# Moving 272 TensorE transposes of an attention + MLP kernel to the DMA crossbar on SyncE's queue

## The chip, the cores and the metric

The kernel runs on one core of one Trainium2 chip. The metric is device time in microseconds (us) of one execution; lower is better. Where a number below comes from several executions it is a median with its range. Each run was profiled too, and the profile gives the "span", from the first to the last counted instruction; it is 1 to 3 us shorter than the time.

The engines are TensorE (PE; its weight loads are PEld), VectorE (DVE), ScalarE (ACT), GpSimd (POOL) and SyncE (SP), which in this kernel only issues DMAs. Lines such as L216 are lines of the kernel's source. The changed kernel has other line numbers than the kernel before, since lines were added.

## The reference

Sliding-window causal attention, then a residual MLP with a layer norm in front:

```python
# q, k, v: (8, 8, 576, 64) = batch, head, position, head dim, float32; window = 64
scores = q @ k.T / sqrt(64);  keep 0 <= i - j < 64
attn = softmax(scores) @ v                       # (8, 8, 576, 64)
x = attn.transpose(0, 2, 1, 3).reshape(8, 576, 512)
xn = (x - mean) / sqrt(var + 1e-6) * g_ln
out = x + relu(xn @ w_ch1) @ w_ch2               # 512 -> 2048 -> 512
```

## The kernel before

The work is cut into nine groups. Group g runs the MLP of batch g's first 512 positions (group 8: the 64 last positions, the "tail", of all eight batches). While PE does the MLP of batch g, the kernel also does the attention of batch g+1 and prepares q, k and v of batch g+2. The MLP of a group is a list of 30 units (16 pieces of layer 1, called `l1` or `hps`, then 14 stages of layer 2), and the other work is placed behind units by slot numbers. The program gives each engine its instructions in the order of these slots, and the timelines below show them run in that order.

Three things are transposed. In the kernel before, PE does it against an identity matrix, and ACT or DVE copies the result out of PSUM: q and k of each batch (`t_main`), q and k of the tails (`t_tail`), and the normalised rows z that feed layer 1 (`zt_step`).

```python
def load_qk(b, half):
    for x, src in enumerate((q, k)):
        t = p_in.tile([128, 1024], FP32, tag=f"qk32_{x}", ...)          # 2 buffers
        ...
        nc.sync.dma_start(                                              # 512 KB, runs of 1 KB
            out=t[:, :].rearrange("p (h m) -> p h m", h=4),
            in_=src[b, 4*half:4*half+4, 0:SM, :].rearrange("h (p j) d -> p h (j d)", j=4))

def t_main(b, x, half, eng=None):
    src = qk16.pop((b, x, half))
    tp = t_tile([128, 8, 128], ...)                                     # PSUM
    for i in range(8):
        nc.tensor.transpose(out=tp[:, i, :], in_=src[:, i], identity=ident16)
    ...
    evac(x if eng is None else eng, dst..., tp...)                      # ACT or DVE copy

def zt_step(g, kb, eng="act"):
    z = zsd.pop((g, kb))
    ...                                                                 # zT[g]: [128, 4, 512] fp16
    ztp = t_tile([128, NKC, 128], ...)
    for kc in range(NKC):
        nc.tensor.transpose(out=ztp[:, kc, :], in_=z[:, 128*kc:128*(kc+1)], identity=ident16)
    dst = zT[g][:, :, 128*kb:128*kb+128]
    nc.scalar.copy(out=dst, in_=ztp)

def l1(hc):                                       # needs ALL of zT[g]
    for kc in range(NKC):
        nc.tensor.matmul(out=hps, lhsT=w1g[:, kc, 128*hc:128*(hc+1)], rhs=zT[g][:, kc, :], ...)

def b_step(g, kb):                                # attention output -> x_norm, pool pxn: 4 buffers
    if kb % 2 == 0:
        x_norm[(g, kb // 2)] = p_xn.tile([128, 2, DM], FP32, tag="xn", ...)
    ...

def store(kb):                                    # the same buffer, after the MLP was added to it
    nc.sync.dma_start(out=out[g, 128*kb:128*kb+128, :], in_=x_norm[(g, kb // 2)][:, kb % 2, :])

# schedule of group g (b = g + 1, n = g + 2); TAILS = {3: [0], 5: [1], 7: [2, 3]}; cut
at((2, 7, 12, 17)[j], z_step, b, j)               # z on POOL, four blocks
at((8, 13, 18, 23)[j], zt_step, b, j)
for i, (x, half) in zip((17, 19, 21, 25), ...): at(i, t_main, n, x, half, 0)
at(17, load_qk, n + 1, 0);  at(18, load_qk, n + 1, 1);  at(23, load_v, n + 1, 0, 4)
# tail i of the next group: load_tail at 5, cast_tail at 24, t_tail at 27 and 29
# its first use: s_mm of the tail at slot 1 of groups 3, 5 and 7
# stores: two in stage "4", two in stage "3" (the last four units)
```

All loads and stores of this schedule and (after the change) all crossbar transposes are issued by SyncE; of the large transfers only the copies that make vB (GpSimd's queue) and one 128 KB store (ScalarE's) are not. The timelines show SyncE issuing in order: an issue that has to wait for its input holds up everything that SyncE would issue after it (experiment 9 shows one such wait, 3.4 us).

The softmax here doesn't subtract the row's maximum and nothing guards it: scores larger than these inputs give would overflow.

Of the kernel before, what the change touches and what calls it, by code (L numbers as in the profile page):

```python
# [11 lines left out]
FP16 = mybir.dt.float16  # L12
# [8 lines left out]
def kernel(  # L21
# [10 lines left out]
    nc = tc.nc  # L32
    B, H, S, D = q.shape
    DM = H * D
    HID = 4 * DM
    SM = 512
# [2 lines left out]
    NHC = HID // 128  # L39
    NHP = H // 2  # L40
    EPS = 1e-6
    scale = 1.0 / (D ** 0.5)

    p_const = ctx.enter_context(tc.tile_pool(name="pconst", bufs=1))
    p_wst = ctx.enter_context(tc.tile_pool(name="pwst", bufs=4))
    p_in = ctx.enter_context(tc.tile_pool(name="pin", bufs=2))
# [25 lines left out]
    def t_tile(shape, name):  # L72
        i = 0 if tbank["shared"] else tbank["n"] % 2
        tbank["n"] = i + 1
        return ps_t.tile(shape, FP16, tag=f"t{i}", name=name)

    qk32, qk16, v32 = {}, {}, {}
    tail32, tail16, tailT, vT = {}, {}, {}, {}
    qkT, vA, vB, pts = {}, {}, {}, {}
    x_norm, zT, mvg, zsd, rstd = {}, {}, {}, {}, {}  # L80

    def load_qk(b, half):
        for x, src in enumerate((q, k)):
            t = p_in.tile([128, 1024], FP32, tag=f"qk32_{x}", name=f"qk32_{x}_{b}_{half}")
            qk32[(b, x, half)] = t
            if b < 2:
                nc.sync.dma_start(  # L87
                    out=t[:, :].rearrange("p (h m) -> p h m", h=H),
                    in_=src[b, :, 256 * half:256 * half + 256, :].rearrange("h (p j) d -> p h (j d)", j=2),
                )  # L90
            else:
                nc.sync.dma_start(
                    out=t[:, :].rearrange("p (h m) -> p h m", h=4),
                    in_=src[b, 4 * half:4 * half + 4, 0:SM, :].rearrange("h (p j) d -> p h (j d)", j=4),
                )
# [12 lines left out]
    def cast_tail(i):  # L108
        tq, tk, tv = tail32.pop(i)
        q16 = p_in.tile([128, H, D], FP16, tag="tq16", name=f"tq16_{i}", bufs=1)  # L110
        k16 = p_in.tile([128, 2, H, D], FP16, tag="qk16_1", name=f"tk16_{i}")
        vt = p_va.tile([128, 2, H, D + 1], FP16, tag="vt", name=f"vt_{i}", bufs=1)
        tail16[i] = (q16, k16)
        vT[i] = vt
        nc.gpsimd.memset(vt[:, :, :, D:D + 1], 1.0)
        nc.gpsimd.tensor_copy(out=q16, in_=tq)
        nc.gpsimd.tensor_copy(out=k16, in_=tk)
        nc.gpsimd.tensor_copy(out=vt[:, :, :, 0:D], in_=tv)

    def cast_qk(b, half):  # L120
        for x in range(2):
            t = qk32.pop((b, x, half))
            dst = p_in.tile([128, 8, 2, D], FP16, tag=f"qk16_{x}", name=f"qk16_{x}_{b}_{half}")
            qk16[(b, x, half)] = dst
            j = 2 if b < 2 else 4
            nc.gpsimd.tensor_copy(  # L126
                out=dst[:, :].rearrange("p (a j) e d -> p a e j d", j=j),
                in_=t[:, :].rearrange("p (a e j d) -> p a e j d", e=2, j=j, d=D),
            )
# [70 lines left out]

    def alloc_qkT(b):
        qkT[b] = [p_qkt.tile([128, NHP, SM + 64 * x], FP16, tag=f"qkT{x}", name=f"qkT{x}_{b}") for x in range(2)]
        nc.gpsimd.memset(qkT[b][1][:, :, 0:64], 0.0)

    def evac(x, out, in_):
        if x == 0:
# [2 lines left out]
            nc.vector.tensor_copy(out=out, in_=in_)  # L209

    def t_main(b, x, half, eng=None):
        src = qk16.pop((b, x, half))
        j = 2 if b < 2 else 4
        tp = t_tile([128, 8, 128], f"tp_{b}_{x}_{half}")
        for i in range(8):
            nc.tensor.transpose(out=tp[:, i, :], in_=src[:, i], identity=ident16)  # L216
        if b < 2:
            c0 = 64 * x + 256 * half
            dst = qkT[b][x][:, :, c0:c0 + 256]
        else:  # L220
            dst = qkT[b][x][:, 2 * half:2 * half + 2, 64 * x:64 * x + 512]
        evac(x if eng is None else eng, dst.rearrange("c h (p j) -> c h p j", j=j),
             tp[:, :].rearrange("c (h j) p -> c h p j", j=j))

    def t_tail(i, x):
        src = tail16[i][x]
        if x == 0:
            tailT[i] = (p_qkt.tile([128, NHP, 128], FP16, tag="tqT", name=f"tqT_{i}", bufs=1),
                        p_qkt.tile([128, 2, NHP, 128], FP16, tag="tkT", name=f"tkT_{i}", bufs=1))
            tp = t_tile([128, NHP, 128], f"tpq_{i}")  # L230
            for hp in range(NHP):
                nc.tensor.transpose(out=tp[:, hp, :], in_=src[:, 2 * hp:2 * hp + 2, :], identity=ident16)
        else:
            tp = t_tile([128, 2, NHP, 128], f"tpk_{i}")
            for r in range(2):
                for hp in range(NHP):
                    nc.tensor.transpose(out=tp[:, r, hp, :], in_=src[:, r, 2 * hp:2 * hp + 2, :], identity=ident16)
        evac(0, tailT[i][x], tp)

    def s_mm(g, j, pe_mask=False):  # L240
        sc = [ps_s.tile([128, NHP, 2, 64], FP32, tag="sc", name=f"sc_{g}_{j}_{par}") for par in range(2)]
        pt = p_pt.tile([128, 2, NHP, 2, 64], FP16, tag="pt", name=f"pt_{g}_{j}")
        pts[(g, j)] = pt
        if pe_mask:
            m = mbias[:, :]
            mb = bass.AP(tensor=m.tensor, offset=m.offset, ap=[m.ap[0], [0, NHP * 2], m.ap[1]])
            for par in range(2):
                nc.tensor.matmul(
                    out=sc[par][:, :].rearrange("p h w i -> p (h w) i"), lhsT=ident16, rhs=mb,
                    start=True, stop=False, skip_group_check=True,  # L250
                )
        for hp in range(NHP):
            for iw in range(2):
                for par in range(2):
                    rows = slice(64 * par, 64 * par + 64)
                    if g == NGRP - 1:
                        lhsT = tailT[j][1][rows, iw, hp, :]
                        rhs = tailT[j][0][rows, hp, 64 * iw:64 * iw + 64]
                    else:
                        w = 2 * j + iw  # L260
                        lhsT = qkT[g][1][rows, hp, 64 * w:64 * w + 128]
                        rhs = qkT[g][0][rows, hp, 64 * w:64 * w + 64]
                    nc.tensor.matmul(out=sc[par][:, hp, iw, :], lhsT=lhsT, rhs=rhs,  # L263
                                     start=not pe_mask, stop=True, skip_group_check=pe_mask)
        for par in range(2):
            nc.scalar.activation(out=pt[:, par], in_=sc[par], func=AF.Exp, bias=0.0, scale=scale)  # L266
# [54 lines left out]
    def zt_step(g, kb, eng="act"):  # L321
        z = zsd.pop((g, kb))
        if g not in zT:
            sfx = "r" if g == NGRP - 1 else ""
            zT[g] = p_grp.tile([128, NKC, 512], FP16, tag="zT" + sfx, name=f"zT_{g}", bufs=1 if sfx else 2)
        ztp = t_tile([128, NKC, 128], f"ztp_{g}_{kb}")
        for kc in range(NKC):
            nc.tensor.transpose(out=ztp[:, kc, :], in_=z[:, 128 * kc:128 * (kc + 1)], identity=ident16)  # L328
        dst = zT[g][:, :, 128 * kb:128 * kb + 128]
        if eng == "act":  # L330
            nc.scalar.copy(out=dst, in_=ztp)  # L331
        else:
            nc.vector.tensor_copy(out=dst, in_=ztp)
# [303 lines left out]
    for g in range(NGRP):  # L637
# [3 lines left out]
        def at(i, f, *a):  # L641
            slots[min(i, len(slots) - 1)].append((f, a))

        b = g + 1
# [78 lines left out]
        if g > 1 and b < B:  # L723
            for j in range(4):
                if j:
                    at((2, 7, 12)[j - 1], s_mm, b, j)
                    at((3, 8, 13)[j - 1], s_mask, b, j)
                at((2, 7, 12, 17)[j], b_step, b, j)
                at((2, 7, 12, 17)[j], z_step, b, j)
                at((8, 13, 18, 23)[j], zt_step, b, j)  # L730
        for n, i in enumerate(TAILS.get(g, ())):
            ts = (10, 11, 14, 20) if n else (1, 2, 5, 11)
            at(ts[0], s_mm, NGRP - 1, i)
# [5 lines left out]
        if g > 1 and n < B:  # L739
            at(16, cast_qk, n, 1)  # L740
            at(20, alloc_v, n)
            at(20, cast_v, n, 0, 2)
            at(21, cast_v, n, 2, 4)
            at(21, alloc_vB, n)
            at(21, make_vB, n)
            for i, (x, half) in zip((17, 19, 21, 25), ((0, 0), (1, 0), (0, 1), (1, 1))):
                at(i, t_main, n, x, half, 0)
            at(27, s_mm, n, 0)
            at(28, s_mask, n, 0)
            if n + 1 < B:  # L750
                at(17, load_qk, n + 1, 0)
                at(18, load_qk, n + 1, 1)
                at(23, load_v, n + 1, 0, 4)
# [53 lines left out]
```

## Time and profile before

| | before |
|---|---|
| time, median of 2 runs | 324.88 us (324.31 to 325.46) |
| span of the profiled run | 322.6 us |
| PE busy | 309.6 us (96%) |
| span less PE busy | 13.0 us |
| PE transposes | 448 |

The page of the kernel before opens with busy time and share of the span by engine, then shows busy tenths in 40 slices of the span. PEclk is the granted TensorE clock in tenths of full speed, DMA the mean busy share of the 16 DMA engines.

```profile
PE 309.6 (96%) x3229; PEld 204.6 (63%) x3229; DVE 204.3 (63%) x388; ACT 176.8 (55%) x292; POOL 164.6 (51%) x251
...
PE   7978999999989999999999999999999999999993
...
PEclk9999999999999999999999999999999999999998
DMA  8999999976089947904598459000570190003013
```

PE is busy in nearly every slice and its clock is full nearly throughout (mean 0.996); no other engine is near its limit. The chain of work that ended last says the same (shares of the span):

```profile
PE 85%; DVE 4%; SPq 3%; DMA 2%; POOL 2%; ACT 1%; issue 0%; ACTq 0%; POOLq 0%
```

So time taken off PE shortens this kernel, provided that PE does not wait for whatever takes the work over. What the transposes cost PE is read from the chain, in order of time (start, us, engine, output, line, count):

```profile
154.37 0.45 PE tp L216 x8
```

Eight transposes take 0.45 us of the chain, 0.056 us each. The groups of instructions (count, then busy us and mean ns of one, then idle before) show 225 ns each for the same instructions; that is how long one lasts, and they overlap, so the mean must not be multiplied by the count:

```profile
L216 PE MATMUL tp<-ident,qk 128*128 128x128 f16 x256 | 20.1, 225 | 0.0
```

The queue that the change uses is SyncE's. This is its timeline from 146 to 170 us (start, us, queue, line, operation, count); the duration is time that SyncE spent on the issue, waiting included:

```profile
147.81 0.39 SPq L92 DMA_DIRECT2D qk<-in_q_dram  x1
148.80 0.39 SPq L92 DMA_DIRECT2D qk<-in_k_dram  x1
...
158.82 4.68 SPq L139 DMA_DIRECT2D v<-in_v_dram  x4
163.68 4.14 SPq L401 DMA_DIRECT2D out_dram<-xn  x4
```

Per group it carries four loads of q and k, four of v and four stores; nothing stands on it that waits for the attention of this group. The list of waits holds one line that becomes important later (total us, times, longest):

```profile
DVE xn L297 <- DMA out_dram<-xn: 2.2, 3, 1.7
```

VectorE may write a new `x_norm` only once the store of the one that lay in that buffer has landed. In the kernel before that costs 2.2 us of DVE time and no visible PE time.

### The profile page before, as it was taken

The numbers are of one execution on the slowest core, as the hardware profiler recorded it, in microseconds if no ns is written. First come the engines' busy times: TensorE is split into PE (matmuls) and PEld (weight loads), VectorE is DVE, ScalarE is ACT, GpSimd is POOL, SyncE is SP. The second block draws the span as 40 slices with busy tenths as digits, with TensorE's granted clock in tenths as the row PEclk, the third lists the DMA queues.
The fourth block names the chain that finished last, engine by engine and source line by source line (L and its number), as shares of the span: only waits on it lengthen the run. The fifth ranks groups of instructions, "written<-read, shape, count | busy, mean of one in ns | idle before, by whom it ended". The sixth has DMA issues, their size and how long they took to land.

```text
span 322.6 us, 7813 instructions
## 1 busy us (share of the span) xinstructions
PE 309.6 (96%) x3229; PEld 204.6 (63%) x3229; DVE 204.3 (63%) x388; ACT 176.8 (55%) x292; POOL 164.6 (51%) x251
## 2 busy tenths in 40 slices
PE   7978999999989999999999999999999999999993
PEld 4556444687544578656964696459755865694582
DVE  0887764666885795489447954896559644751643
ACT  2576624487346754876457647775486157405600
POOL 7678765423991689079705982598036506200000
PEclk9999999999999999999999999999999999999998
DMA  8999999976089947904598459000570190003013
GB/s 194 282 385 259 363 306 295 264 267 133 35 276 227 207 139 204 241 2 133 173 259 183 132 168 259 26 2 2 171 182 2 24 241 33 0 2 131 0 36 98
DMA packets 85639, 51.08 MB, mean 158 GB/s; under 512 B 55682, under 2 KB 76674, under 8 KB 85603
## 3 DMA queue, kind: packets, MB, share of 16 engines
q1 hardware_dynamic: 84816, 48.11, 55.6%
q0 software_dynamic: 640, 2.33, 3.1%
q8 instruction: 25, 0.41, 0.5%
q10 hardware_dynamic: 146, 0.13, 0.1%
q14 instruction: 12, 0.09, 0.1%
HBM read 38.80 MB, written 9.44 MB: 150 GB/s over the span
## 4 chain that ended last, share of the span: by engine, by line
PE 85%; DVE 4%; SPq 3%; DMA 2%; POOL 2%; ACT 1%; issue 0%; ACTq 0%; POOLq 0%
PE hps L363 33%; PE pA L435 11%; PE pC L435 8%; PE pB L435 8%; PE hph L484 6%; PE ch L375 4%; PE xps L291 4%; PE tp L216 3%; PE sc L263 3%; DMA w1s<-in_moe_w_ch_dram 2%; PE ztp L328 2%; SPq L139 2%; POOL w1g L188 1%; PE ch L499 1%; DVE wT L532 1%; SPq L87 1%
## 5 line engine op out<-in xcount | busy, mean ns | idle before, releaser
L363 PE MATMUL hps<-zT,w1g 128*128 128x512 f16 x480 | 112.0, 379 | 0.0
L367 ACT ACTIVATE hrT<-hps 128x512 f16<-128x512 f32 x120 | 71.9, 599 | 35.1 <-PE hps L363 31.6
L363 PEld LDWEIGHTS <-w1g 128*128 128x128 f16 x480 | 44.1, 98 | 47.0 <-issue 1.0
L316 POOL TENSOR_SCALAR rsz<-mvg 128x1 f32<-128x1 f32 x28 | 12.2, 437 | 76.5 <-DVE mvg L302 75.5
L266 ACT ACTIVATE pt<-sc 128x512 f16<-128x512 f32 x72 | 39.0, 595 | 14.6 <-PE sc L263 13.1
L435 PEld LDWEIGHTS <-sS 128*128 128x128 f16 x448 | 43.0, 98 | 4.7
L207 ACT COPY qkT<-tp 128x1024 f16<-128x1024 f16 x26 | 26.2, 1012 | 33.6 <-PE tp L216 32.4
L126 POOL CAST qk<-qk 128x1024 f16<-128x1024 f32 x32 | 33.7, 1070 | 9.5 <-DMA qk<-in_q_dram 4.9
L442 DVE TENSOR_TENSOR xn<-pA,xn 128x512 f32<-128x512 f32 x28 | 19.2, 686 | 26.1 <-PE pA L435 17.4
L331 ACT COPY zT<-ztp 128x512 f16<-128x512 f16 x36 | 21.1, 586 | 26.5 <-PE ztp L328 26.1
L435 PEld LDWEIGHTS <-hrT 128*128 128x128 f16 x336 | 32.3, 98 | 5.0
L294 DVE RECIPROCAL rcp<-xps 128x8 f32<-128x8 f32 x36 | 7.4, 205 | 34.3 <-PE xps L291 34.1
L414 DVE TENSOR_TENSOR sS<-hrT 128x512 f16<-128x512 f16 (+1 forms) x42 | 21.4, 510 | 10.2 <-ACT hrT L367 10.2
L297 DVE TENSOR_TENSOR xn<-xps,rcp 128x512 f32<-128x512 f32 x36 | 24.9, 692 | 3.3 <-DMA out_dram<-xn 2.2
L435 PE MATMUL pA<-wT,sS 128*128 128x256 f16 x224 | 26.9, 273 | 0.0
L435 PE MATMUL pC<-w2s,sS 128*128 128x256 f16 x224 | 26.8, 273 | 0.0
L273 DVE TENSOR_TENSOR pt<-pt,mask 128x1024 f16<-128x1024 f16 x28 | 21.2, 762 | 8.6 <-ACT pt L266 8.5
L484 PE MATMUL hph<-zT,w1g 128*128 128x256 f16 x192 | 23.6, 273 | 2.5 <-ACT zT L331 1.1
L299 DVE BATCH_NORM_STATS2 stats<-xn 128x6 f32<-128x512 f32 x36 | 25.0, 695 | 1.2
L319 POOL TENSOR_SCALAR z<-xn,rsz 128x512 f16<-128x512 f32 x28 | 23.4, 836 | 2.9
L375 PE MATMUL ch<-w2s,hrT 128*128 128x512 f16 x96 | 23.7, 380 | 0.1
L484 PEld LDWEIGHTS <-w1g 128*128 128x128 f16 x192 | 18.0, 98 | 5.8 <-issue 2.2
(85 smaller groups left out, 437.2 us busy)
## 6 DMA issues: line engine op xcount, KB each, us to landing
out_dram<-xn SPq DMA_DIRECT2D x34, 256.0 KB, 3.6
qk<-in_q_dram SPq DMA_DIRECT2D x16, 512.0 KB, 4.8
qk<-in_k_dram SPq DMA_DIRECT2D x16, 512.0 KB, 5.9
v<-in_v_dram SPq DMA_DIRECT2D x32, 256.0 KB, 6.2
w2s<-in_moe_w_ch_dram SPq DMA_DIRECT2D x12, 512.0 KB, 5.6
w1s<-in_moe_w_ch_dram SPq DMA_DIRECT2D x4, 512.0 KB, 7.3
tk<-in_k_dram SPq DMA_DIRECT2D x8, 256.0 KB, 4.4
tv<-in_v_dram SPq DMA_DIRECT2D x8, 256.0 KB, 5.1
```

What stands on the lines that cost most here:

```text
L126: nc.gpsimd.tensor_copy(out=dst[:, :].rearrange("p (a j) e d -> p a e j d", j=j), in_=t[:, :].rearrange("p (a e j d) -> p a e j d", e=2, j ...
L207: nc.scalar.copy(out=out, in_=in_)
L266: nc.scalar.activation(out=pt[:, par], in_=sc[par], func=AF.Exp, bias=0.0, scale=scale)
L297: nc.vector.tensor_tensor(out=xn, in0=xps[:, :, 0:D], in1=rcp_b, op=ALU.mult)
L299: nc.vector.bn_stats(out=stats, in_=xv)
L319: nc.gpsimd.tensor_scalar(out=z, in0=xv, scalar1=rs, scalar2=nm, op0=ALU.mult, op1=ALU.add)
L363: nc.tensor.matmul(out=hps, lhsT=w1g[:, kc, 128 * hc:128 * (hc + 1)], rhs=zT[g][:, kc, :], start=(kc == 0), stop=(kc == NKC - 1),)
L367: nc.scalar.activation(out=hrT[:, hc, :], in_=hps, func=AF.Relu, bias=0.0, scale=1.0)
L375: nc.tensor.matmul(out=ch[kb], lhsT=hrT[:, hc, 128 * kb:128 * (kb + 1)], rhs=w2s[:, hc, :], start=(hc == 0), stop=(hc == NHC - 1),)
L414: nc.vector.tensor_tensor(out=o, in0=x, in1=y, op=op)
L435: nc.tensor.matmul(out=bank[which][:, p, :], lhsT=a[:, c, 128 * p:128 * p + 128], rhs=wv[:, c, :], start=(first and p == 0 and c == 0), st ...
L484: nc.tensor.matmul(out=hps[:, e], lhsT=w1g[:, kc, 128 * hc:128 * (hc + 1)], rhs=zT[g][:, kc, 256 * half:256 * half + 256], start=(kc == 0) ...
```

## The change

The intent: give PE less to do. From batch 4 on q and k are transposed by the DMA crossbar, one transpose of 512 KB for each of the two (`XQ = 4`); so are all tails, and the z of groups 3 to 8 (`XZ = 3`). That takes 272 of the 448 transposes from PE and 48 copies from ACT. For these transposes q and k lie in another layout, so their loads become eight of 256 KB in runs of 256 bytes in place of four of 512 KB in runs of 1 KB. The z transposes are placed one or two slots earlier, the q, k transposes all behind unit 17.

```diff
+    XQ = 4
+    XZ = 3
@@ load_qk
+            elif b >= XQ:
+                for c in range(2):
+                    s0 = 256 * half + 128 * c
+                    nc.sync.dma_start(
+                        out=t[:, 512 * c:512 * c + 512].rearrange("p (h d) -> p h d", h=H),
+                        in_=src[b, :, s0:s0 + 128, :].rearrange("h s d -> s h d"),
+                    )
@@ t_main
+        if b >= XQ:
+            if half == 0:
+                dst = flat(b, x)[:, 64 * x:64 * x + NHP * SM]
+                nc.sync.dma_start_transpose(out=dst.rearrange("p (a t) -> p a t", t=128),
+                                            in_=cast16[x][:, :, :, :].rearrange("p a c m -> p (a c m)"))
+            return
@@ t_tail, for q (x == 0); the same for k into tailT[i][1]
+            if XQ < B:
+                nc.sync.dma_start_transpose(out=tailT[i][0], in_=src[:, :, :].rearrange("p h d -> p (h d)"))
+                return
@@ zt_step
+        if g >= XZ:
+            nc.sync.dma_start_transpose(out=zT[g][:, :, 128 * kb:128 * kb + 128], in_=z)
+            return
@@ schedule
-                at((8, 13, 18, 23)[j], zt_step, b, j)
+                at((6, 11, 16, 22)[j], zt_step, b, j)
-            for i, (x, half) in zip((17, 19, 21, 25), ((0, 0), (1, 0), (0, 1), (1, 1))):
+            for i, (x, half) in zip((17, 17, 17, 17) if n >= XQ else (17, 19, 21, 25),
+                                    ((0, 0), (1, 0), (0, 1), (1, 1))):
```

Cut from the diff: static fp16 tiles `cast16` as the source of the transposes, the casts that write them in the new order, and the flat addressing of `qkT` in the score matmuls.

More of the change, by code (lines that the diff above doesn't have):

```diff
@@ L77 @@
     qk32, qk16, v32 = {}, {}, {}
+    cast16 = [p_const.tile([128, NHP, 4, 128], FP16, tag=f"cast16_{x}", name=f"cast16_{x}") for x in range(2)]
     tail32, tail16, tailT, vT = {}, {}, {}, {}
@@ L110, in cast_tail @@
         q16 = p_in.tile([128, H, D], FP16, tag="tq16", name=f"tq16_{i}", bufs=1)
-        k16 = p_in.tile([128, 2, H, D], FP16, tag="qk16_1", name=f"tk16_{i}")
+        k16 = cast16[1][:, 0:2].rearrange("p r c (e d) -> p r (c e) d", d=D)
         vt = p_va.tile([128, 2, H, D + 1], FP16, tag="vt", name=f"vt_{i}", bufs=1)
@@ L122, in cast_qk @@
             t = qk32.pop((b, x, half))
-            dst = p_in.tile([128, 8, 2, D], FP16, tag=f"qk16_{x}", name=f"qk16_{x}_{b}_{half}")
+            if b >= XQ:
+                nc.gpsimd.tensor_copy(
+                    out=cast16[x][:, :, 2 * half:2 * half + 2, :].rearrange("p a c m -> p c a m"),
+                    in_=t[:, :].rearrange("p (c a m) -> p c a m", c=2, a=NHP),
+                )
+                continue
+            dst = cast16[x][:, 2 * half:2 * half + 2, :, :].rearrange("p a c (e d) -> p (a c) e d", d=D)
             qk16[(b, x, half)] = dst
@@ L202, in alloc_qkT, with flat @@
         qkT[b] = [p_qkt.tile([128, NHP, SM + 64 * x], FP16, tag=f"qkT{x}", name=f"qkT{x}_{b}") for x in range(2)]
-        nc.gpsimd.memset(qkT[b][1][:, :, 0:64], 0.0)
+        if b < XQ:
+            nc.gpsimd.memset(qkT[b][1][:, :, 0:64], 0.0)
+        else:
+            nc.gpsimd.memset(qkT[b][1][:, 0, 0:64], 0.0)
+    def flat(b, x):
+        return qkT[b][x][:, :, :].rearrange("p h m -> p (h m)")
     def evac(x, out, in_):
@@ L211, in t_main @@
     def t_main(b, x, half, eng=None):
+        if b >= XQ:
+            if half == 0:
[3 more added lines that the diff above has]
+            return
         src = qk16.pop((b, x, half))
@@ L233, in t_tail @@
         else:
+            if XQ < B:
+                nc.sync.dma_start_transpose(out=tailT[i][1][:, :, :, :].rearrange("p r h t -> p (r h) t"),
+                                            in_=src[:, :, :, :].rearrange("p r h d -> p (r h d)"))
+                return
             tp = t_tile([128, 2, NHP, 128], f"tpk_{i}")
@@ L258, in s_mm @@
                         rhs = tailT[j][0][rows, hp, 64 * iw:64 * iw + 64]
+                    elif g >= XQ:
+                        c0 = SM * hp + 64 * (2 * j + iw)
+                        lhsT = flat(g, 1)[rows, c0:c0 + 128]
+                        rhs = flat(g, 0)[rows, c0:c0 + 64]
                     else:
@@ L325, in zt_step @@
             zT[g] = p_grp.tile([128, NKC, 512], FP16, tag="zT" + sfx, name=f"zT_{g}", bufs=1 if sfx else 2)
+        if g >= XZ:
+            nc.sync.dma_start_transpose(out=zT[g][:, :, 128 * kb:128 * kb + 128], in_=z)
+            return
         ztp = t_tile([128, NKC, 128], f"ztp_{g}_{kb}")
```

## The prediction

> **What bounds it now.** The page: PE is busy 309.6 of 322.6 us (96%) and holds 85% of the chain of waits; DVE has 63%, ACT 55%, POOL 51%. In the stretches from 131 to 305 us PE is 100% busy; groups 2 to 5 take about 33 us each. So a PE instruction removed there shortens the kernel, if its replacement arrives in time. The DMA share is about 0.76 between 148 and 198 us, lower later.
>
> **Removed.** 272 of 448 PE transposes (128 of q and k, 48 of tails, 96 of z) and 48 ACT copies. On the chain eight transposes cost 0.45 us, so PE loses 272 x 0.056 = 15.3 us, all on the critical path: about 3 us in each of groups 2 to 5, 1.6 and 1.1 in 6 and 7. ACT loses about 37 us, off the path.
>
> **Added.** On SyncE's queue: 8 transposes of 512 KB, 4 of 256 KB, 28 of 128 KB or so. The Trainium skill (DMA: Bandwidth & Descriptors, Latency and other measured facts) gives 261 GB/s for a DMA transpose; no run here shows it yet. Estimate: 2 us for 512 KB, 0.5 us for 128 KB, plus about 2 us latency (loads here start moving about 2 us after issue). The q, k loads of batches 4 to 7 break into 256-byte pieces: traced packets take 18 ns for 256 B, 46 ns for 1 KB, and v's 256-byte traffic moves about 800 packets/us, so one batch's q and k (8192 packets) take about 10 us, where the 2 MB took about 5.5 us.
>
> **Order on the queue decides.** SyncE issues in order, and each DMA engine takes a queue's descriptors in order (same page, Queues, rings and completion order). In groups 2 to 4 the order is: transposes of q, k; eight loads of the next batch; the transpose of z's last block; v loads; stores; tail transposes.
> - The casts that feed the q, k transposes end about 21 us into a group (POOL's timeline: 120.2, start 98.9). Add 4 to 5 us of transposes, 10 us of loads, 2 us of vB copies on POOL's queue, 1.5 us for z: the last zT block lands 37 to 39 us into the group. The next group's first matmul needs it; PE would arrive after 30.
> - tkT, needed two units (2 us) into groups 3, 5, 7, stands behind v (5 us), stores (2.8 us) and tqT: another 6 to 8 us of stall in groups 3 and 5, 3 to 4 in group 7.
>
> Sum: -15 saved, +24 (three z stalls of 8), +18 (tails): about +27.
>
> **Prediction:** 350 us, range 326 to 378. Faster 0.10, within 2% 0.08, slower 0.82.
>
> **What would show it.** PE busy falls by about 15 us yet the span grows; new PE waits at the first hps of groups 3, 4, 5 released by DMA zT<-z, and at the tail sc of groups 3, 5, 7 released by DMA tkT; eight load issues on SyncE between the q, k transposes and the fourth z transpose; groups without loads (5, 6) 2 to 3 us shorter; ACT busy 37 us less.
>
> **What would make it wrong.** Loads and transposes overlapping rather than draining in order, or 256-byte loads faster than v's: the z stall vanishes and 310 to 318 us follows. Transposes far slower than 261 GB/s (3x: 512 KB in 6 us), or long issue on SyncE: up to 390 us. A granted clock that falls in the new PE pauses adds more.

## The result

| | before | after |
|---|---|---|
| time, median (range, 2 runs each) | 324.88 us | 371.79 us (370.40 to 373.19) |
| span of the profiled run | 322.6 us | 371.4 us |
| PE busy | 309.6 us | 307.4 us |
| span less PE busy | 13.0 us | 64.0 us |
| PE transposes | 448 | 176 |
| ACT busy | 176.8 us | 143.4 us |
| packets of 256 bytes | 53,248 | 120,832 |
| mean granted TensorE clock | 0.996 | 0.919 |

The changed kernel is slower: ratio 1.144, 95% interval 1.124 to 1.165. Here and below, a ratio is the mean time of one kernel's fast runs over that of the other's fast runs of the same rounds, so it is not quite the ratio of the medians that are quoted. The single runs (experiments 1, 2, 4 and 7) have no known state, and a difference from them of a few us alone would show nothing; their traces carry the argument.

The sum closes exactly: PE busy changed by -2.2 us, PE's idle time by +51.0 us, together the +48.8 us of the span. The same lines of the page as before, now of the changed kernel:

```profile
PE 307.4 (83%) x2957; PEld 192.6 (52%) x2957; DVE 201.7 (54%) x388; ACT 143.4 (39%) x244; POOL 163.2 (44%) x251
...
PE   7989999999899804999349981389999975999994
...
PEclk9999999999999975699959996579999996999998
DMA  8999999654999999016999199911695194203013
...
PE 55%; SPq 16%; DVE 11%; DMA 6%; issue 6%; POOL 4%; ACT 1%; POOLq 0%; ACTq 0%
```

PE has holes, and in and after each hole the granted clock falls. The DMA share is 0.9 or more over most of the middle. In the chain PE fell from 85% to 55%, and SyncE's queue, 3% before, has 16%. PE's timeline shows the holes (in brackets: idle just before, and what ended it):

```profile
139.54 3.57 PE L405 MATMUL hps<-zT,w1g 128*128 128x512 f16 x8 [11.01 <-issue]
148.26 0.61 PE L302 MATMUL sc<-tqT,tkT 64*128 64x64 f16 x16 [5.15 <-DMA tkT<-cast]
...
190.72 4.80 PE L405 MATMUL hps<-zT,w1g 128*128 128x512 f16 x11 [10.99 <-issue]
...
233.96 3.57 PE L405 MATMUL hps<-zT,w1g 128*128 128x512 f16 x8 [10.04 <-DMA zT<-z]
242.95 0.61 PE L302 MATMUL sc<-tqT,tkT 64*128 64x64 f16 x16 [5.42 <-DMA tkT<-cast]
...
310.90 0.61 PE L302 MATMUL sc<-tqT,tkT 64*128 64x64 f16 x16 [6.98 <-DMA tkT<-cast]
```

Six pauses, 49.6 us in all: 32.0 us at the first layer-1 matmul of groups 3, 4 and 5, which needs the whole of zT, and 17.6 us at the tail scores of groups 3, 5 and 7. For two of the three zT pauses the profile names no releaser ("issue"). But the last zT transpose of group 4's rows landed at 190.63 us and PE went on at 190.72; for group 3's it was issued at 135.62, the last of the 16 increments of its semaphore is recorded at 139.45, and PE went on at 139.54.

Why zT comes so late is seen in SyncE's timeline of the changed kernel from 169 to 195 us, to be compared with that of the kernel before:

```profile
169.14 1.19 SPq L366 DMA_TRANSPOSE zT<-z  x1
170.42 4.47 SPq L237 DMA_TRANSPOSE qkT<-cast  x2
174.95 1.60 SPq L97 DMA_DIRECT2D qk<-in_q_dram  x2
176.59 2.11 SPq L97 DMA_DIRECT2D qk<-in_k_dram  x2
178.75 6.04 SPq L97 DMA_DIRECT2D qk<-in_q_dram  x2
184.83 1.96 SPq L97 DMA_DIRECT2D qk<-in_k_dram  x2
186.89 1.64 SPq L366 DMA_TRANSPOSE zT<-z  x1
188.63 2.98 SPq L155 DMA_DIRECT2D v<-in_v_dram  x4
191.70 2.73 SPq L443 DMA_DIRECT2D out_dram<-xn  x4
```

The transposes of z's third block and of its last block stand 17.8 us apart, with the q, k transposes and the next batch's eight loads between them. The last block of z was ready long before; POOL's timeline:

```profile
173.16 1.01 POOL L358 TENSOR_SCALAR z<-xn,rsz 128x512 f16<-128x512 f32 x1
```

It was made at 174.17 and its transpose issued at 186.89, 12.7 us later (in group 2: 122.98 and 135.62). The Trainium skill (DMA: Bandwidth & Descriptors, Queues, rings and completion order) says that on each DMA engine descriptors are consumed in ring order; this trace agrees: the transpose issued at 186.89 landed 3.7 us later, at 190.63, behind the last of those loads (190.08), where the median zT transpose needs 2.5. The eight loads keep SyncE itself for 11.7 us, up to 6 us for one pair of issues, where one of the four loads of the kernel before took it 0.4 us. In that stretch (174.95 to 186.80) the view of windows gives a DMA share of 1.13 (I read 1 or more as full engines). So order puts z behind the loads, and loads that fill the DMA engines make the place behind them expensive.

The view of DMA issues of the changed kernel gives the median time in us from issue to landing of the transposes of z and of q, k (the lines give no size; by the tiles they are 128 KB and 512 KB):

```profile
zT<-z SPq DMA_TRANSPOSE x24, 2.5
...
qkT<-cast SPq DMA_TRANSPOSE x8, 4.5
```

From 128 KB in 2.5 us to 512 KB in 4.5 us, 384 KB (393,216 bytes) more take 2.0 us longer, which is 197 GB/s. This slope includes SyncE's own time for the issue (median 1.2 us for zT, 2.1 for qkT), so it is not the rate of the transfer alone. From the list of waits of the changed kernel, for comparison with the experiments, the line of the `x_norm` buffers:

```profile
DVE xn L336 <- DMA out_dram<-xn: 0.6, 1, 0.6
```

Two things in the sum are less plain.

- PE busy fell by only 2.2 us although 15.3 us of transposes had gone. The granted clock was 0.5 in four stretches of the trace, in which PE was busy 25.4 us together. At full clock that would have been 12.7 us (this takes all PE work as going with the clock). So -15.3 and +12.7 leave 0.4 us of the measured -2.2 open.
- A group that loads nothing did get shorter. Group 6 runs 28.8 us from its first to its next group's first layer-1 matmul in the changed kernel (273.2 to 302.0), 30.5 us in the kernel before (231.3 to 261.8). So PE does profit where nothing stands in the queue.

### The profile page after: what moved, and what is told of

Its sections match the earlier page's. It is cut to its first block, busy times and chain, and to the rows that moved or that the text cites. A ratio compares the mean times of both kernels' runs of the same rounds, so it can differ in the third digit from the quotient of the medians.

```text
span 371.4 us, 7324 instructions
## 1 busy us (share of the span) xinstructions
PE 307.4 (83%) x2957; PEld 192.6 (52%) x2957; DVE 201.7 (54%) x388; ACT 143.4 (39%) x244; POOL 163.2 (44%) x251
## 4 chain that ended last, share of the span: by engine, by line
PE 55%; SPq 16%; DVE 11%; DMA 6%; issue 6%; POOL 4%; ACT 1%; POOLq 0%; ACTq 0%
PE hps L405 26%; SPq L97 6%; PE pA L477 6%; PE hph L526 5%; PE pC L477 4%; PE pB L477 4%; DMA tkT<-cast 4%; SPq L155 3%; PE ch L417 3%; PE xps L330 3%; PE sc L302 3%; SPq L443 2%; DMA w1s<-in_moe_w_ch_dram 2%; DVE stats L338 2%; DVE xn L336 2%
## 5 line engine op out<-in xcount | busy, mean ns | idle before, releaser
L405 PE MATMUL hps<-zT,w1g 128*128 128x512 f16 x480 | 119.6, 405 | 32.0 <-issue 22.0
L405 PEld LDWEIGHTS <-w1g 128*128 128x128 f16 x480 | 46.7, 102 | 89.7 <-issue 44.4
L477 PEld LDWEIGHTS <-hrT 128*128 128x128 f16 x336 | 32.5, 98 | 5.4
L312 DVE TENSOR_TENSOR pt<-pt,mask 128x1024 f16<-128x1024 f16 x28 | 23.4, 843 | 14.9 <-ACT pt L305 14.8
L358 POOL TENSOR_SCALAR z<-xn,rsz 128x512 f16<-128x512 f32 x28 | 24.4, 870 | 2.9
L142 POOL CAST cast<-qk 128x1024 f16<-128x1024 f32 x16 | 16.6, 1044 | 9.9 <-DMA qk<-in_q_dram 4.8
L526 PEld LDWEIGHTS <-w1g 128*128 128x128 f16 x192 | 18.1, 98 | 5.1 <-issue 2.2
L356 POOL TENSOR_TENSOR rsz<-rsz,mhalf 128x1 f32<-128x1 f32 x28 | 19.3, 688 | 2.3
L330 PEld LDWEIGHTS <-pt 128*64 128x64 f16 x576 | 12.5, 112 | 14.4 <-issue 7.8
```

Of the source, the lines that this page charges most:

```text
L312: nc.vector.tensor_tensor(out=ptv, in0=ptv, in1=mb, op=ALU.mult)
L330: nc.tensor.matmul(out=xps[64 * r:64 * r + 64, h, :D + 1], lhsT=pt[:, par, hp, r, :], rhs=rhs, start=True, stop=True)
L358: nc.gpsimd.tensor_scalar(out=z, in0=xv, scalar1=rs, scalar2=nm, op0=ALU.mult, op1=ALU.add)
L405: nc.tensor.matmul(out=hps, lhsT=w1g[:, kc, 128 * hc:128 * (hc + 1)], rhs=zT[g][:, kc, :], start=(kc == 0), stop=(kc == NKC - 1),)
L477: nc.tensor.matmul(out=bank[which][:, p, :], lhsT=a[:, c, 128 * p:128 * p + 128], rhs=wv[:, c, :], start=(first and p == 0 and c == 0), st ...
L526: nc.tensor.matmul(out=hps[:, e], lhsT=w1g[:, kc, 128 * hc:128 * (hc + 1)], rhs=zT[g][:, kc, 256 * half:256 * half + 256], start=(kc == 0) ...
```

## The experiments

The theory after the first look was about order. SyncE issues in order, so a transpose that waits for its input holds the loads behind it, and z's last transpose and the tail transposes get behind loads, `v` loads and stores that PE does not need yet. Rivals: the clock (the pauses slow PE and that sets the pace); the crossbar and the 256-byte loads fill the DMA engines, so that any order is slow; and a plain sum, in which each pause can be taken away by itself. Expectations are quoted as they were before each run. "Before" was 325.07, 324.59 and 324.88 us (medians of 7, 7 and 11 runs).

### 1. The tails back on PE

```diff
 def t_tail(i, x):
-            if XQ < B:        # both places
+            if False:
```

> The changed kernel with the tails back on PE; q, k and z stay on the crossbar. Queue-order theory (a transpose waits for all that SyncE issued before it): the three PE waits at the tail scores (5.2, 5.4, 7.0 us) go, the three waits at the first hps of groups 3, 4, 5 (11, 11, 10 us) stay; PE gains 2.7 us of transposes and loses some half-clock time: about 351 us (346 to 356). If the tails' waits were not caused by their own transposes: no change, about 371.

Measured: 350.62 us (1 run), span 348.9, clock 0.95. The tail pauses are gone (17.6 us) and the time fell by 21.2 us. The zT pauses stayed at 9.5 to 10.5 us each; from the list of waits (total us, times, longest), the two of them whose releaser the profile names:

```profile
PE hps L405 <- DMA zT<-z: 20.2, 2, 10.5
```

The tails' part is what the trace had said, and a bit more; that the higher clock gives the rest is not shown apart.

### 2. z back on PE, the rest on the crossbar

```diff
-    XZ = 3
+    XZ = 9
```

> The changed kernel with z back on PE; q, k and tails stay on the crossbar. Queue-order theory: the waits for zT go, but in groups 3 and 5 the tail transpose still stands behind the same loads and stores, lands at nearly the same time, and its wait grows from 5 to about 15 us; only group 4 gains its 11 us: about 362 us (356 to 367). Additive rival (each kind of transpose costs its own stall): all of the 32 us and some clock time come back, about 339 us.

Measured: 390.99 us (1 run), span 389.3. Both expected times missed: the kernel got slower by 19 us, though the three zT pauses were gone. From the list of waits:

```profile
PE sc L302 <- DMA tkT<-cast: 39.2, 4, 16.1
PE ztp L370 <- POOL z L358: 28.6, 16, 11.1
DVE xn L336 <- DMA out_dram<-xn: 10.5, 1, 10.5
```

The tail waits grew from 18.4 us in the changed kernel's list to 39.2 us, which refutes the plain sum: PE arrives sooner at the tail scores, and the queue is not sooner. The longest is 16.1 us, near the 15 of the queue-order theory. Two further things come in. The slots (6, 11, 16, 22) put z's transposes so early that PE, which now does them, waits for POOL's z; that is a fault of this experiment. And one long wait ends with an output store: DVE could not write `x_norm`, since the store of the buffer had not landed. PE then waits for z, which is made from it.

### 3. Only q and k on the crossbar

```diff
-    XZ = 3
+    XZ = 9
 def t_tail(i, x):
-            if XQ < B:        # both places
+            if False:
```

> Only q, k of batches 4 to 7 on the crossbar, with their 256-byte loads; tails and z on PE. Queue-order theory: nothing that PE needs soon stands behind the eight loads, so no wait over 2 us and 128 PE transposes (7.2 us) are saved: 318 us (315 to 322). Bandwidth rival (the DMA engines cannot carry the 256-byte loads and 1 MB of transposes per group, in whatever order): waits stay, over 330 us.

Measured: 372.21 us (371.07 to 374.58, 4 runs), ratio 1.148 (1.143 to 1.154). It missed by 54 us: with no z and no tail on the queue, the kernel is as slow as with all of them. The time lies where the bandwidth rival had put it (over 330); what speaks against that rival as the main cause comes only with experiment 10, where the same transposes and bytes give 323 us. The waits:

```profile
DVE xn L336 <- DMA out_dram<-xn: 30.6, 3, 10.5
PE ztp L370 <- POOL z L358: 28.2, 14, 11.1
```

So there is a third thing behind the loads, which I had not named: the stores. The three pauses come again, now from `x_norm` buffers whose stores SyncE issues only after the loads. In the changed kernel this is hidden (0.6 us), because PE has already been held by zT for as long. The early z slots are still in this run, so it needed a cleaner repetition.

### 4. The same with the slots of the kernel before

```diff
 # on top of experiment 3
-                at((6, 11, 16, 22)[j], zt_step, b, j)
+                at((8, 13, 18, 23)[j], zt_step, b, j)
```

> As e3 (q, k alone on the crossbar) but with the PE transposes of z back at their slots of before (8, 13, 18, 23), because e3 put them at the earlier slots and PE then waited in line for z, 1.8 and 1.1 us per group. Those six pairs go (17 us); the three waits of about 10 us behind the store of xn stay if the stores' place in SyncE's queue is their cause: about 355 us (350 to 360). If they were a result of the early slots: about 320.

Measured: 355.69 us (1 run), span 353.8, as expected. 16.5 us of experiment 3's loss were the early slots. The rest is seen in SyncE's timeline of this run:

```profile
120.01 4.71 SPq L237 DMA_TRANSPOSE qkT<-cast  x2
124.77 1.61 SPq L97 DMA_DIRECT2D qk<-in_q_dram  x2
...
142.19 2.64 SPq L443 DMA_DIRECT2D out_dram<-xn  x4
```

And in DVE's timeline:

```profile
146.36 0.69 DVE L336 TENSOR_TENSOR xn<-xps,rcp 128x512 f32<-128x512 f32 x1 [10.99 <-DMA out_dram<-xn]
```

The stores are issued at 142 us, behind loads that only began at 124.8 because the transposes stood before them. The first two landed at 145.60 and 146.23 us, and 0.1 us later DVE, idle for 11 us, goes on. It happens three times, once in each group whose loads come before its stores in this way; the three waits are 33.5 us together, the longest 11.4. PE stands still with DVE, at the attention output `xps`, which DVE has to read before PE may go on; two lines of the list of waits (the releaser named is the last one in time):

```profile
PE xps L330 <- POOL rsz L355: 21.0, 2, 10.6
PE xps L330 <- DVE pt L312: 9.1, 1, 9.1
```

### 5. Stores from ScalarE's queue

```diff
 # on top of experiment 4
-            nc.sync.dma_start(out=out[g, ...], in_=x_norm[...])
+            (nc.scalar if g > 1 else nc.sync).dma_start(out=out[g, ...], in_=x_norm[...])
```

> As e9, with the output stores of groups 2 on issued from ScalarE, so on another hardware queue: same bytes, same DMA engines, but not behind the loads. If the order in SyncE's queue is the cause, the three waits of xn for its store go: about 323 us (318 to 331; ScalarE pays some issue time). If the DMA engines are simply short of bandwidth, stores share them and come late all the same: over 345.

Measured: 350.55 us (349.85 to 352.31, 4 runs), ratio 1.080 (1.077 to 1.084), 5.1 us less than experiment 4. DVE no longer waits for stores, but the waits moved to ScalarE; two of the three lines in its list of waits:

```profile
ACT tkT L229 <- DMA out_dram<-xn: 11.6, 2, 6.6
...
ACT hrT L409 <- DMA qk<-in_q_dram: 6.6, 1, 6.6
```

ScalarE stood still before it issued stores. The trace's instruction records show why: the program's DMAs use eight completion semaphores in turn, and an issue waits for the DMA that used its semaphore eight issues earlier. The store issued at 136.14 us, for example, waits on the semaphore of the k load issued at 128.20. So a store on ScalarE waited for loads after all, and held up the work behind it. Whether the stores by themselves would have come through past the loads, or have shared the engines with them, this run does not tell. It is inconclusive on that, although the time lies where the bandwidth rival had put it (over 345).

### 6. Everything on the crossbar, other order

```diff
-            if n + 1 < B:
-                at(17, load_qk, n + 1, 0);  at(18, load_qk, n + 1, 1);  at(23, load_v, n + 1, 0, 4)
+        if g > 2 and n < B:                       # the same loads, early in the NEXT group
+            at(1, load_qk, n, 0);  at(3, load_qk, n, 1);  at(12, load_v, n, 0, 4)
-                at(27, t_tail, i, 0);  at(29, t_tail, i, 1)
+                at(26, t_tail, i, 0);  at(26, t_tail, i, 1)
```

> All transposes of the change stay on the crossbar; only the order on SyncE's queue changes: the loads of the next batch's q, k and v move from the end of a group to the start of the next, and both tail transposes go before the stores. Same bytes, same packets. Queue-order theory: the waits at the first hps and at the tail scores fall under 2 us each, the clock stays granted, PE saves its 15 us: about 312 us (308 to 318). Bandwidth rival: the waits stay in some form, over 330 us.

Measured: 336.39 us (335.38 to 338.41, 3 fast runs; a fourth, 341.86, was slow), ratio 1.037 (1.032 to 1.042). The new places, with the same transposes and the same bytes, give back 35.4 of the 46.9 us. Moving the loads changes their order and also spreads them over time; this run does not tell the two apart. Of the zT pauses 0.6 us is left; new, shorter ones came, at the scores (list of waits):

```profile
PE sc L302 <- DMA qkT<-cast: 7.3, 1, 7.3
PE sc L302 <- DMA tkT<-cast: 7.0, 3, 4.3
PE sc L302 <- issue: 5.6, 2, 2.8
```

It missed 312 us all the same, and lies where the bandwidth rival was expected (over 330). PE is busy 301.2 of 333.7 us: 8.4 us less than before and not 15, at a mean clock of 0.972, and 32.5 us idle, 19.5 more than before; the listed pauses are 20.5 us. The longest, 7.3 us, is in group 4. In the view of windows, this is group 4's stretch, from 158 to 200 us (stretch, length, then busy us with instruction count for PE, PEld, DVE, ACT, POOL; the last three are clock, DMA share, GB/s):

```profile
158.00:200.00 42.00, 31.89 (x319) 20.55 (x318) 22.55 (x43) 13.57 (x24) 19.66 (x32) 0.91 1.10 199
```

By the same reading the engines were full for 42 us, while 199 GB/s were moved. The transposed q, k of this group come late. I take that for the rival's share of the cause, but order is not out of it: the four v loads and one z transpose are still issued (185.8 to 190.5 us) ahead of these q, k transposes, whose casts had ended at 186.2. No run puts the v loads behind them.

### 7. The clock held up

```diff
+        def hold(n, name):    # n matmuls into an unused PSUM tile, results never read
+            ...
 # 44 of them ahead of groups 3, 4, 5; 24 ahead of each of the first three tail scores
```

> The changed kernel plus idle matmuls on PE just where it waits: 44 before the first hps of groups 3, 4, 5 and 24 before the tail scores of tiles 0, 1, 2. They take no time that PE did not stand idle, and results do not use them. If the halved granted clock after each pause is a cost of its own, the clock stays at 1.0 and the time falls by about 9 us, to about 362 (359 to 366). If the half-clock time is hidden (the DMA sets the pace anyway): under 3 us.

Measured: 367.94 us (1 run), span 366.2, mean clock 0.995. The page's clock line is now:

```profile
PEclk9999999999999998999999999999999999999999
```

With a full clock almost everywhere the time fell by 3.9 us only (one run; against the two runs of the changed kernel it is 2.5 and 5.2). That lies between the two expectations, 9 us and under 3. PE still waited for zT (4.2 us in three places) and at the tail scores (4.4 us in four), so the extra matmuls did not hold it up there. The half clock inflates PE's busy time by 12.7 us but sets only some 4 us of the time. My reading is that a slow PE mostly arrives later at its next wait, since the queue sets the pace. The clock as the main cause is refuted; its exact share is not known from one run.

### 8. Only the 256-byte loads, all transposes on PE

```diff
-    XZ = 3
+    XZ = 9                    # tails on PE and z slots (8, 13, 18, 23) too
 def t_main(b, x, half, eng=None):
         if b >= XQ:
-            ... dma_start_transpose ...
+            ... eight nc.tensor.transpose of cast16[x][:, 2*half + a, c, :], one evac ...
```

> The 256-byte layout of the q, k loads of batches 4 to 7 alone: no crossbar at all, PE transposes everything, slots as before. If the finer loads by themselves made most of the loss: over 345 us. If they matter only because the queue also waits for casts and carries transposes: the eight loads start some 6 us earlier than in the changed kernel, the stores land 2 to 4 us later than before, and xn waits for them a little in groups 3 to 5: 325 to 336 us.

Measured: 328.99 us (328.56 to 329.53, 4 runs), ratio 1.013 (1.010 to 1.016). The new layout by itself costs 4 us, inside the expected range, and no 10 us pause comes with it. The trace shows PE busy 1.6 us more and its gaps 2.6 us more. Among its waits are four of the q, k transposes for POOL's cast, 3.4 us together (the longest 1.0), which the kernel before does not have: in the new layout a transpose needs the casts of both halves. So most of the gaps come from the layout of the cast and not from the loads; the 1.6 us stay open. What matters here is what it is not: loads in 256-byte runs do not bring the pauses unless a transpose holds the queue in front of them.

### 9. Only z on the crossbar

```diff
-    XQ = 4
+    XQ = 8                    # q, k and tails on PE, loads of 1 KB runs
```

> Only z of groups 3 to 8 on the crossbar; q, k, tails as before. PE saves 96 transposes, 5.4 us. With 1 KB loads that do not wait for casts, the last z transpose lands before the next group starts: no wait over 1 us, about 319.5 us (317 to 323). If the crossbar itself costs PE: over 325.

Measured: 334.44 us (331.90 to 336.17, 6 runs), ratio 1.028 (1.024 to 1.032). It missed by 15 us, and lies where a cost of the crossbar itself had been expected (over 325). The smallest of the transposes, with loads as before, still costs. (The early slots are in this run too.) SyncE's timeline of this run:

```profile
113.86 6.40 SPq L366 DMA_TRANSPOSE zT<-z  x2
120.31 0.58 SPq L102 DMA_DIRECT2D qk<-in_q_dram  x1
...
133.91 2.85 SPq L443 DMA_DIRECT2D out_dram<-xn  x4
```

And its list of waits:

```profile
DVE xn L336 <- DMA out_dram<-xn: 12.3, 3, 4.9
```

SyncE spent 6.4 us on two transposes, 3.4 of them waiting for the second one's z, which was made at 119.04 us. The first q, k loads behind them were issued at 120.31 instead of 114.06 us, the stores at 133.91 instead of 129.70, and DVE waited for stores 12.3 us; PE waited 9.0 us at `xps` after it. So the store pauses come without any 256-byte q, k load: here the queue's time before a transpose is what delays the loads and stores behind it. That the transfers themselves add nothing is not tested.

### 10. Only q and k, loads in the next group

```diff
 # on top of experiment 4
-                at(17, load_qk, n + 1, 0);  at(18, load_qk, n + 1, 1);  at(23, load_v, n + 1, 0, 4)
+        if g > 2 and n < B:
+            at(1, load_qk, n, 0);  at(3, load_qk, n, 1);  at(12, load_v, n, 0, 4)
```

> Only q, k on the crossbar (as e9), with the loads of q, k, v moved to the start of the next group (as e5). If order was the whole cause, q, k gain their 7.2 us: about 318 us (315 to 322). If bandwidth limits as in e5, where 256-byte packets kept the engines busy for all of group 4 and the transposed q, k came 3 to 7 us late: waits at the scores of groups 3 to 5, 322 to 332.

Measured: 323.13 us (322.75 to 323.46, 4 runs), ratio 0.994 (0.992 to 0.997). Against experiment 4 only the place of the loads differs, and it takes away 32.6 us. The time lies just above the order theory's 315 to 322 and in the range given for the bandwidth limit, of whose waits in groups 3 to 5 only one came. PE busy is 304.4 us, 5.2 less than before, and one pause remains, 3.6 us at the scores of group 4, ended by a q, k transpose (190.6 to 194.2 us). The windows show the stretch before it:

```profile
158.00:190.00 32.00, 32.00 (x338) 21.67 (x336) 22.03 (x42) 15.70 (x28) 18.52 (x29) 1.00 1.02 209
```

The columns are those of experiment 6. The DMA share is 1.02: the engines are full here too, at 209 GB/s, while PE is still 100% busy. Here too the four v loads (179.55 to 184.5 us) are issued just ahead of the q, k transposes.

### 11. z and tails, stores ahead of the v loads

```diff
-    XQ = 4
+    XQ = 8
-            if XQ < B:        # both places in t_tail
+            if True:
-                at(23, load_v, n + 1, 0, 4)
+                at(29, load_v, n + 1, 0, 4)
-                at(27, t_tail, i, 0);  at(29, t_tail, i, 1)
+                at(26, t_tail, i, 0);  at(26, t_tail, i, 1)
```

> z and tails on the crossbar, q and k on PE with their 1 KB loads as before; both tail transposes issued before the stores, the v loads after them. 144 PE transposes (8 us) are saved and little stands before what PE needs: about 318 us (315 to 323) if order and the 256-byte loads made the loss. If a crossbar transpose itself costs PE a wait wherever it stands: over 330.

Measured: 327.90 us (327.48 to 328.75, 4 runs), ratio 1.010 (1.008 to 1.013). No wait for stores is left; it missed 318 us by a tail pause of 5.1 us in group 7 (and 1.3 us in group 3) and by 6.8 us of the trace at half clock. In group 7 the last tail's six loads are issued ahead of `tqT` and `tkT` (slots 25 and 26 of group 6).

### 12. The same, the last tail's loads behind the transposes

```diff
 # on top of experiment 11
-                at(25, load_tail, i)
+                at(28, load_tail, i)
```

> e14 with one more swap: in group 6 the loads of the last tail go after the transposes of the one before it. In e14 these six loads stood before it and PE waited 5.1 us at its scores, followed by 6.8 us at half clock. That wait should fall under 1.5 us: about 319 us (316.5 to 322). If it stays, the tail transpose is late for another reason: about 327.

Measured: 322.69 us (321.37 to 325.41, 5 fast runs; a sixth, 326.96, was slow), ratio 0.994 (0.990 to 0.998). Group 7's pause fell from 5.1 to 2.9 us in the profiled run (325.41 us) and not under the expected 1.5; the others are 1.3 and 1.2, and 6.8 us at half clock remain. The time is 3.7 us above the expected 319; the remaining pauses and the half clock are what the trace shows for it.

Experiments 10 and 12 are the best of all: 0.6% under the kernel before, with intervals that leave out 1 (for experiment 12, without its slow run). No version tried beats the kernel before by more.

## Why the prediction was right

It gave 350 us, 326 to 378, and slower with 0.82; measured were 371.79 us. Direction and mechanism held, the size was 22 us short. The upper end of its range was argued with transposes of 6 us for 512 KB; they took 4.5, so the missing time came from elsewhere. Point by point:

- **"So a PE instruction removed there shortens the kernel, if its replacement arrives in time."** Right on both counts. Group 6, which loads nothing, is 1.7 us shorter; "the z stall" and the tails' are where the replacement came late. ACT busy fell by 33.4 us, predicted 37. The prediction had put groups 5 and 6 at 2 to 3 us shorter; group 5 ran 39.2 us instead of 33.3, because the tail pause and part of the half clock fall in it.
- **"Order on the queue decides."** Right, and tested: experiment 6 changes nothing but the places on the queue and takes back 35.4 of 46.9 us; experiment 10 against 4 takes 32.6 us.
- **Tails, "+18".** 17.6 us, right in sum, and that partly by luck: the shares were 5.2, 5.4 and 7.0 us in groups 3, 5 and 7, not 6 to 8 twice and 3 to 4. Experiments 11 and 12, in their own order, show that the last tail's loads in front of the transposes lengthen group 7's pause; the prediction had not counted these.
- **"+24 (three z stalls of 8)".** This is the term that was mis-sized: 32.0 us. In group 2 the last zT block landed 40.6 us into the group (139.45 less 98.87), not "37 to 39", while PE arrived at 29.6, a little before the predicted 30. The steps of those 40.6 us: the q, k transposes were issued at 20.4 us (predicted 21), took 5.0 us of the queue's time (predicted 4 to 5), the eight loads 11.4 (predicted 10, and 2 for copies of v on another queue, which I don't find as a step of their own), and zT landed 3.8 us after its issue (predicted 1.5). So it was above all the last transpose, behind loads still in flight. The 261 GB/s that the prediction took from the Trainium skill (DMA: Bandwidth & Descriptors, Latency and other measured facts) is not tested by these runs: the slope was 197 GB/s with the issue time in it, and 512 KB took 4.5 us from issue to landing.
- **"A granted clock that falls in the new PE pauses adds more."** It was named and put at nothing in the sum. It added 12.7 us to PE's busy time and so ate most of the predicted -15; by experiment 7, some 4 us (one run) of the kernel's time come back when the clock is held. The named thing was real, and removing it is worth little.
- **What it didn't see: the stores.** The prediction counted zT and tails as what stands behind the loads. The output stores stand there too, and the `x_norm` buffers wait for them. In the changed kernel that shows 0.6 us. It became the main loss in experiment 4, where z and tails were off the queue, and a part of it in experiments 2, 3 and 9, so the simple form of my own theory, "take away zT and tails and the gain appears", fell in experiment 3.
- **What it didn't see: the engines fill.** In group 4 the DMA share reached 1.10 and 1.02 in experiments 6 and 10. Once order is mended, this is where the remaining pauses are seen next to full engines. That bandwidth causes them is argued from this, not tested: no run has fewer bytes, and none puts the v loads behind the transposes.

The sum in spans, predicted +27, measured +48.8, so 21.8 us more. The six pauses are 49.6 us where 42 were predicted (+7.6, nearly all of it zT's 8.0). The half clock is 12.7 us of PE busy time where nothing was counted. The remaining 1.5 us are the small pauses and the 0.4 us left open above, less the 0.3 us by which the transposes were worth more than 15. The 12.7 us (half of the 25.4 us that PE was busy at half clock) are an arithmetic part of this sum, not a cause that can be removed for that amount, as experiment 7 shows.

Left open: where the 1.6 us of PE time in experiment 8 come from; whether stores on another queue would overtake the loads if they did not share completion semaphores with them; and whether order or the spreading of the loads over time does more, since no run moves z's last transpose ahead of the loads of the same group and leaves the rest.

## What to carry to other kernels

Before moving work onto a DMA queue, write down the order of that queue with the time at which each entry's input is ready: an entry that waits holds up every load and every store behind it, and the stores hold buffers. Put what the next stage needs first ahead of the bulk loads that nobody needs yet; here that placement alone was worth 35 us, while the PE work removed was 15 us. And when one wait is taken away, look for the one that it was hiding before counting the gain.

## What the Trainium skill lacked or had wrong

- DMA: Bandwidth & Descriptors (Latency and other measured facts) gives 261 GB/s for a DMA transpose with a non-contiguous middle dimension and about 350 to 400 when contiguous. Between on-chip tiles in this kernel the step from 128 KB to 512 KB was 197 GB/s, but with the issue time in it, so it neither agrees nor refutes. What the section lacks is a latency for a transpose: here 128 KB took 2.5 us from issue to landing and 512 KB 4.5.
- The same page (Rules for kernel authors) says that a transpose next to ordinary DMAs needs nothing. Every run here gave a correct result, which agrees. What the page lacks is the cost in time of sharing one queue with loads and stores: with z's transposes alone SyncE spent 6.4 us on two of them (experiment 9), and in the changed kernel PE then waited 10 to 11 us in each of three groups.
- No page that I read says that output stores behind loads on one queue keep their buffers from being used again. That was 33.5 us of waiting in experiment 4.
- TensorE: Matmul & The Clock Gate (Part 1) gives half clock after about 3.4 us idle and full clock after about 3.4 us busy. The trace of the changed kernel agrees on the two values. Its times scatter: at the four lowerings PE had been idle for 5.4, 5.4, 2.1 and 4.1 us (for example from 128.53, lowered at 133.91), and at the returns it had been busy since its last pause for 6.1, 4.6, 3.6 and 3.9 us (for example from 190.72, full at 195.34). The page does not say that such a stretch need not cost its full time where something else sets the pace: 12.7 us of PE busy time, some 4 us of the kernel's (one run).
